# Windowed attention with sinks and a highway layer: rows in pairs for the 32x32 transpositions of q, and the last two batches loaded whole

## The chip, the cores and the metric

The kernel runs on one core of a Trainium2 chip. The metric is the device time of one execution in microseconds (us); the time shown for a kernel is the median of several runs. The profile is of one execution, and it has that execution's own time beside the span that it covers.

A core has five engines with queues of their own: TensorE (PE in the profile; its weight loads are PEld), VectorE (DVE), ScalarE (ACT), GpSimd (POOL) and SyncE (SP). Each works through its own instructions in order. POOL, SP and ACT also issue DMA transfers.

## The reference

```python
def _attn_ref(q, k, v, n_sink, window):          # q, k, v: [4, 8, 768, 64]; n_sink 4, window 128
    B, H, S, D = q.shape
    scores = np.matmul(q, k.transpose(0, 1, 3, 2)) / np.sqrt(D)
    pos = np.arange(S)
    rel = pos[:, None] - pos[None, :]
    keep = (pos[None, :] < n_sink) | ((rel >= 0) & (rel < window))
    scores = np.where(keep, scores, -1000000000.0)
    a = np.exp(scores - np.max(scores, axis=-1, keepdims=True))
    a = a / (np.sum(a, axis=-1, keepdims=True) + 1e-09)
    return np.matmul(a, v)

def _moe_ref(x, w_h, w_t, b_t):                  # x: [3072, 512], the heads side by side
    H = np.maximum(x @ w_h, 0.0)
    T = 1.0 / (1.0 + np.exp(-(x @ w_t + b_t)))
    return T * H + (1.0 - T) * x
```

All inputs and the output are float32. The kernel works in float16 behind its loads.

## The kernel before

The 4 batches of 768 tokens make 24 tiles of 128 tokens, six to a batch. One loop (`for n in range(N + 2)`, L471) is a software pipeline over these tiles: in iteration n the kernel makes the scores of key tile n and their exponentials, multiplies the values of tile n-1, normalises and transposes tile n-1, and runs the gate and the hidden product of tile n-2. The closing elementwise work of a tile (`complete`: half a tanh, a product, a sum and the store) comes five or six iterations after its scores, by the table `completed` (L448); iteration 13 closes two tiles, and so do iterations 21 to 23. The order of instructions on each engine is that in which the Python code issues them (`_keep_traced_order`). Nothing is moved by a planner.

**Layout of q and k.** The 8 heads are taken as two groups `hg` of four, and the four heads of a group lie on the four quarters of the partitions (`G` = 4, 32 partitions each). POOL loads q and k (L109) and the DMA casts them to float16. A batch is cut in segments: three of 256 tokens for batches 0 and 1, two of 384 for batches 2 and 3. Within a segment, partition r of a quarter holds `run` = 8 or 12 consecutive tokens, all 64 numbers of each. One DMA brings one segment, of q or of k, for the two heads of one quarter; so a segment of q takes four DMAs, and all of batches 1 to 3 takes 56, of which eight come ahead of the table `loads`.

**The transpositions.** `transpose_qk` (L125) reads the float16 data as 4-byte words, two numbers of a head side by side. VectorE transposes blocks of 32 partitions by 32 words: the word moves to the partition, and the 32 partition rows become the free index. Row r of a block belongs to token `r * run + m`, so that consecutive words that one block writes are `run` words apart: 32 bytes for the thirds, 48 bytes for the halves. The result `tr[b]` is, on each partition, for q and k and each `hg`, the tokens in order with the two numbers (`e` = 0, 1) side by side: 4 bytes from token to token. Thirds are done in one instruction for both `hg` (512 words per partition), halves in one per `hg` (384 words).

**Who reads it.** `scores` (L279) takes, for each `hg`, `e` and quarter, 128 tokens of k as weights and up to 256 tokens of q as moving operand, a row group of 32 each, four of them side by side in the array. `sink_scores` (L293) takes q against the four sink keys, and `sink_keys` (L253) puts these keys together from `tr`. 

**Order.** A table `units` says behind which iteration's `norm` VectorE transposes which piece: for batch 1 at iterations 5, 5, 6, 7, 8, 9; for batch 2 at 10, 10, 11, 11, 12, 13, 14, 14; for batch 3 at 16, 16, 17, 17, 18, 19, 20, 20. Batch 2 is first used by `scores(12)`, batch 3 by `scores(18)`; with halves, the second half is first needed in iterations 14 and 15 (and 20 and 21), by the sinks' scores and by key tile 3. The table `loads` says how many DMAs POOL issues in iterations 2 to 16: 4, 4, 4, 4, 3, 3, 3, 3, 2, 3, 3, 3, 3, 3, 3. On POOL an iteration's order is: cast of v(n) (L142), the DMAs of `loads`, the sum that closes a tile (L414), and at the first two tiles of a batch the sinks' keys and values. The values of tile n-1 need the cast of the iteration before. On VectorE the order is: reciprocal and product of `norm` (L349, L351), the transpositions, `diff` (L403), and `gate_value` and `gated` (L384, L408). PE needs the result of `diff` of one iteration before the hidden product of the next can write `ps_h`, which exists once.

## Time and profile before

| | us |
|---|---|
| median of 3 runs | 115.75 |
| lowest and highest of them | 114.94 and 116.42 |
| the profiled execution | 114.55 |
| its span | 112.8 |
| PE busy | 98.4 |
| VectorE busy | 87.5 |
| POOL busy | 87.2 |
| ScalarE busy | 76.6 |

The span begins with the first instruction and ends with the last; the execution's time has 1.75 us more, outside the span. Shares of busy time are means over stages with different limits. Iterations can be told in the timeline of VectorE: each has one reciprocal (L349), that of iteration 1 at 14.39 us, of iteration 24 at 103.34 us. "Chain" means the chain of work that ended last, followed back from the end. A line such as "3.11 DMA nat<-in_k_dram" in it is the time from a DMA's issue to its landing; x4 is the number of instructions that a row merges.

### The profile page before, as it was taken

What the parts mean: (1) busy time and instruction counts of PE and PEld (TensorE: products, weight loads), DVE (VectorE), ACT (ScalarE), POOL (GpSimd) and SP (SyncE); (2) the same over time, 40 slices, a digit from 0 to 9 for tenths busy, and PEclk for the clock granted to TensorE, in tenths of its full rate; (3) what the DMA queues carried; (4) which work ended last, traced back from release to release, by engine and by line L of the source; (5) the groups of instructions that cost most, each with busy time, mean ns of one, the idle gap of its engine ahead of it and who ended that gap; (6) DMA issues with size and microseconds to landing.
All of it is one profiled execution on the core that took longest, in us unless ns stands there. A gap on an engine that the chain in (4) does not pass through costs nothing.

```text
span 112.8 us, 3577 instructions
## 1 busy us (share of the span) xinstructions
PE 98.4 (87%) x1414; PEld 51.5 (46%) x1414; DVE 87.5 (78%) x184; ACT 76.6 (68%) x95; POOL 87.2 (77%) x141
## 2 busy tenths in 40 slices
PE   5986389899989998999999979999999999977900
PEld 2322246345435454655455535644555566523500
DVE  6796587535677986889998998699777979999660
ACT  4476639985557786788587868687678987842520
POOL 6899997249599499997899999999758965866100
PEclk9999999999999999999999999999999999999998
DMA  3999999999999749989998999899994503324222
GB/s 97 222 234 214 210 201 224 192 204 242 212 241 150 112 139 233 256 193 237 203 207 205 224 239 261 166 209 210 242 259 131 162 6 136 143 99 176 103 111 75
DMA packets 36704, 20.81 MB, mean 185 GB/s; under 512 B 27340, under 2 KB 33232, under 8 KB 36688
## 3 DMA queue, kind: packets, MB, share of 16 engines
q1 hardware_dynamic: 29680, 13.50, 46.6%
q0 software_dynamic: 6848, 6.82, 38.6%
q10 hardware_dynamic: 160, 0.26, 0.8%
q8 instruction: 11, 0.18, 0.7%
q14 instruction: 5, 0.04, 0.1%
HBM read 21.11 MB, written 6.29 MB: 243 GB/s over the span
## 4 chain that ended last, share of the span: by engine, by line
PE 39%; DVE 22%; POOL 14%; DMA 14%; issue 7%; DVEq 1%; POOLq 0%
POOL nat L109 11%; PE ps_h L390 9%; DMA wh<-in_moe_w_h_dram 9%; PE ps_z L371 8%; DVE tr L125 7%; PE ps_s L279 5%; DMA nat<-in_k_dram 5%; DVE DD L403 4%; DVE TH L384 4%; PE ps_av L341 4%; PE ps_av L338 3%; PE ps_s L272 3%; DVE DD L408 2%; PE ps_av L362 2%; DVE X L351 2%
## 5 line engine op out<-in xcount | busy, mean ns | idle before, releaser
L327 ACT ACTIVATE E<-ps_s,ebias 128x2048 f16<-128x2048 f32 (+1 forms) x24 | 43.8, 1825 | 12.6 <-PE ps_s L279 12.6
L414 POOL TENSOR_TENSOR O<-DD,X 128x512 f32<-128x512 f16 x22 | 25.4, 1156 | 10.1 <-DVE DD L408 4.2
L390 PE MATMUL ps_h<-wh,XT 128*128 128x512 f16 (+1 forms) x96 | 27.4, 375 | 0.2 <-DMA wh<-in_moe_w_h_dram 0.2
L125 DVE STREAM_TRANSPOSE tr<-nat 128x384 f32<-128x384 f32 (+1 forms) x28 | 25.7, 957 | 2.3 <-DMA nat<-in_k_dram 1.9
L109 POOL DMA_DIRECT2D nat<-in_k_dram x40 | 21.9, 554 | 5.5 <-DMA wh<-in_moe_w_h_dram 3.7
L371 PE MATMUL ps_z<-wt,XT 128*128 128x512 f16 x96 | 24.6, 379 | 0.0
L403 DVE SCALAR_TENSOR_TENSOR DD<-ps_h,X 128x512 f16<-128x512 f32 (+1 forms) x24 | 16.2, 673 | 8.2 <-PE ps_h L390 8.1
L367 ACT COPY XT<-ps_av 128x512 f16<-128x512 f16 x24 | 14.1, 586 | 7.8 <-PE ps_av L362 5.0
L378 ACT ACTIVATE TH<-ps_z 128x512 f16<-128x512 f32 x24 | 14.2, 592 | 7.4 <-PE ps_z L371 7.4
L109 POOL DMA_DIRECT2D nat<-in_q_dram x32 | 17.8, 562 | 0.8 <-DMA wt<-in_moe_w_t_dram 0.7
L351 DVE TENSOR_TENSOR X<-ps_av,rec 128x512 f16<-128x512 f32 x24 | 16.6, 692 | 1.0 <-DVE rec L349 0.2
L341 PE MATMUL ps_av<-v,E 128*128 128x65 f16 x192 | 14.1, 194 | 1.9 <-DVE v L142 1.8
L279 PE MATMUL ps_s<-tr 32*128 32x256 f16 (+1 forms) x384 | 14.5, 262 | 1.0 <-DVE tr L125 0.8
L341 PEld LDWEIGHTS <-E 128*128 128x128 f16 x192 | 11.8, 98 | 3.0 <-issue 3.0
L338 PE MATMUL ps_av<-v,E 128*128 128x65 f16 x160 | 12.7, 195 | 0.0
L408 DVE TENSOR_TENSOR DD<-DD,TH 128x512 f16<-128x512 f16 x24 | 11.9, 495 | 0.8
L338 PEld LDWEIGHTS <-E 128*128 128x128 f16 x160 | 10.2, 97 | 4.9 <-issue 4.9
L362 PE MATMUL ps_av<-ident,X 128*128 128x128 f16 x96 | 9.4, 221 | 3.2 <-DVE X L351 3.0
L142 POOL CAST v<-V 128x512 f16<-128x512 f32 x19 | 12.0, 633 | 0.0
L390 PEld LDWEIGHTS <-XT 128*128 128x128 f16 x100 | 8.7, 98 | 6.9 <-issue 0.7
L362 PEld LDWEIGHTS <-X 128*128 128x128 f16 x96 | 5.7, 97 | 12.2 <-DVE X L351 12.2
L371 PEld LDWEIGHTS <-XT 128*128 128x128 f16 x96 | 7.8, 98 | 6.0 <-ACT XT L367 0.3
(62 smaller groups left out, 100.9 us busy)
## 6 DMA issues: line engine op xcount, KB each, us to landing
V<-in_v_dram SPq DMA_DIRECT2D x24, 256.0 KB, 5.2
out_dram<-O SPq DMA_DIRECT2D x23, 256.0 KB, 2.8
nat<-in_k_dram POOLq DMA_DIRECT2D x24, 64.0 KB, 4.5
nat<-in_q_dram POOLq DMA_DIRECT2D x16, 96.0 KB, 4.2
nat<-in_k_dram POOLq DMA_DIRECT2D x16, 96.0 KB, 4.5
nat<-in_q_dram POOLq DMA_DIRECT2D x16, 64.0 KB, 4.9
first<-in_q_dram SPq DMA_DIRECT2D x6, 128.0 KB, 3.7
wt<-in_moe_w_t_dram POOLq DMA_DIRECT2D x1, 512.0 KB, 6.7
```

The costliest lines, as they stand in the source:

```text
L109: engine.dma_start(out=into[32 * g:32 * g + 32].rearrange("p hg m d -> p hg (m d)"), in_=(q, k)[which][b, :, t0:t0 + nt, :].rearrange("(hg ...
L125: dve.transpose(out=dst, in_=src)
L279: last = pe.matmul(ps_s[:, g, hg, 0:nq * P], lhsT=tr[b][rows, 1, hg, c * P:(c + 1) * P, e], rhs=tr[b][rows, 0, hg, c * P:(c + nq) * P, e], ...
L327: act.activation(out=E[n][:, :, :, 0:nq * P], in_=ps_s[:, :, :, 0:nq * P], func=AF.Exp, bias=ebias, scale=SCALE)
L338: pe.matmul(slot, lhsT=E[n - 1][:, g, hg, P:2 * P], rhs=v_of(n - 1)[:, h, :], start=first, stop=False, skip_group_check=True)
L341: pe.matmul(slot, lhsT=E[n][:, g, hg, 0:P], rhs=v_of(n)[:, h, :], start=first, stop=True, skip_group_check=True)
L351: dve.tensor_tensor(out=X[n], in0=av[:, :, :, 0:D], in1=rec.unsqueeze(3).to_broadcast([P, HG, G, D]), op=ALU.mult)
L362: pe.transpose(xt[:, kc // 2, (kc % 2) * P:(kc % 2 + 1) * P], x[:, kc * P:(kc + 1) * P], ident)
L371: pe.matmul(ps_z, lhsT=XT[n][:, kc * P:(kc + 1) * P], rhs=wt[:, kc, :], start=False, stop=(kc == KC - 1), skip_group_check=True)
L390: pe.matmul(into, lhsT=XT[n][:, kc * P:(kc + 1) * P], rhs=wh[:, kc, cols], start=(kc == 0), stop=(kc == KC - 1), skip_group_check=True)
L403: dve.scalar_tensor_tensor(out=DD[n][:, cols], in0=ps_h[:, cols] if h is None else h, scalar=0.0, in1=flat(X[n], cols), op0=ALU.max, op1=A ...
L414: eng.tensor_tensor(out=O[n][:, cols], in0=DD[n][:, cols], in1=flat(X[n], cols), op=ALU.add)
```

## The change

Three things change together.

1. For batches 0 and 1 (`b < SPLIT`) the loads and pieces are the same thirds. The transposition of k is the same. That of q puts rows 2x and 2x+1 of a block side by side: the two words that the two rows give are written at neighbouring addresses, the next pair 64 bytes on. In `tr` the tokens of q are then no longer in order; the readers take them through a pattern (x, y, m), in runs of 8 tokens with 8 bytes from token to token.
2. For batches 2 and 3 one tile holds the whole batch. Partition 32g + 2r + i holds 48 consecutive tokens of head `4i + g`: the rows of a quarter alternate between its two heads. One DMA brings one head of q or of k, 16 partitions of 12 KB read and 6 KB written each (before: 64 pieces of 3 KB read and 1.5 KB written). The number of DMAs stays 56 for batches 1 to 3, and their size 96 KB for batches 2 and 3. The transposition writes the words of the two heads side by side, and `tr` has the two `hg` inside the token: 8 bytes from token to token for q and k. An instruction takes 16 of the 48 tokens of every row, 512 words per partition, three for q and three for k of a batch (before: four and four of 384 words). Each of the three of k needs all eight DMAs of k, and a batch's first scores need all six.
3. The order: batch 2 is transposed at iterations 9, 10, 10 (q) and 11, 11, 11 (k), batch 3 at 14, 15, 15 (q) and 16, 17, 17 (k). The loads come as all of q, then all of k; POOL issues 4 in each of iterations 2 to 9 and then 2, 3, 3, 3, 3, 2, the last in iteration 15.

```diff
+    RUN = SEG // 32
+    SPLIT = 2
+    WHOLE = S // 16
+    nat = [[data.tile([P, 2, HG, RUN, D], FP16, ...) for i in range(NSEG)] for b in range(SPLIT)] + [
+           [data.tile([P, 2, WHOLE, D], FP16, tag=f"nat{b}", name=f"nat{b}")]
+           for b in range(SPLIT, B)]
+    tr = [data.tile([P, 2, HG, S, 2] if b < SPLIT else [P, 2, S, HG, 2], FP16,
+                    tag=f"tr{b}", name=f"tr{b}") for b in range(B)]
...
     def load_part(b, i, g, which, into=None, engine=pool):
...
+        else:
+            engine.dma_start(
+                out=nat[b][0][32 * g + i:32 * g + 32:HG, which].rearrange("p m d -> p (m d)"),
+                in_=(q, k)[which][b, G * i + g].rearrange("(r m) d -> r (m d)", m=WHOLE))
...
-        src = nat[b][i][:, which, hgs].bitcast(FP32).rearrange("p hg m i -> p hg m i")
-        dst = tr[b][:, which, hgs].bitcast(FP32).rearrange("p hg t e -> p hg (t e)")[
-            :, :, t0:t0 + nt].rearrange("p hg (r m) -> p hg m r", m=run)
+    def transpose_qk(b, i, which, parts=NSEG):
+        if b < SPLIT:
+            src = nat[b][i][:, which].bitcast(FP32)
+            dst = tr[b][:, which].bitcast(FP32).rearrange("p hg t e -> p hg (t e)")[
+                :, :, i * SEG:(i + 1) * SEG]
+            if which == 0:
+                dst = dst.rearrange("p hg (x m y) -> p hg m x y", m=RUN, y=2)
+                src = src.rearrange("p hg m (x y) -> p hg m x y", y=2)
+            else:
+                dst = dst.rearrange("p hg (r m) -> p hg m r", m=RUN)
+        else:
+            ms = slice(i * WHOLE // parts, (i + 1) * WHOLE // parts)
+            src = nat[b][0][:, which, ms].bitcast(FP32).rearrange("p m (x y) -> p m x y", y=HG)
+            dst = tr[b][:, which].rearrange("p t hg e -> p t (hg e)").bitcast(FP32).rearrange(
+                "p (x m) y -> p m x y", m=WHOLE)[:, ms]
         dve.transpose(out=dst, in_=src)
+
+    def queries(b, hg, e, t0, nt, rows=slice(0, P)):
+        if b >= SPLIT:
+            return tr[b][rows, 0, t0:t0 + nt, hg, e]
+        return tr[b][rows, 0, hg, t0:t0 + nt, e].rearrange(
+            "p (x m y) -> p x y m", m=RUN, y=2)
+
+    def keys_of(b, hg, e, t0, nt, rows=slice(0, P)):
+        if b >= SPLIT:
+            return tr[b][rows, 1, t0:t0 + nt, hg, e]
+        return tr[b][rows, 1, hg, t0:t0 + nt, e]
...
-                                     lhsT=tr[b][rows, 1, hg, c * P:(c + 1) * P, e],
-                                     rhs=tr[b][rows, 0, hg, c * P:(c + nq) * P, e],
+                                     lhsT=keys_of(b, hg, e, c * P, P, rows),
+                                     rhs=queries(b, hg, e, c * P, nq * P, rows),
...
-            at = (10, 10, 11, 11, 12, 13, 14, 14) if b == 2 else (16, 16, 17, 17, 18, 19, 20, 20)
+            at = (9, 10, 10, 11, 11, 11) if b == 2 else (14, 15, 15, 16, 17, 17)
             for u, n in enumerate(at):
-                i, which, hg = u // 4, u // 2 % 2, u % 2
-                units.setdefault(n, []).append((b, i, which, slice(hg, hg + 1)))
+                units.setdefault(n, []).append((b, u % NSEG, u // NSEG))
...
+    issues += [(b, i, g, which) for b in range(SPLIT, B) for which in range(2)
+               for g in range(G) for i in range(HG)]
-    for n, count in zip(range(2, 17), [4] * 4 + [3, 3, 3, 3, 2, 3, 3, 3, 3, 3, 3]):
+    for n, count in zip(range(2, 16), [4] * 8 + [2, 3, 3, 3, 3, 2]):
```

38 lines of the change are left out of this document (18 added, 20 removed).

## The prediction

> **What bounds the kernel now.** I read the page first: engines, slices, and the chain of waits by engine.
>
> ```profile
> span 112.8 us, 3577 instructions
> ...
> PE 98.4 (87%) x1414; PEld 51.5 (46%) x1414; DVE 87.5 (78%) x184; ACT 76.6 (68%) x95; POOL 87.2 (77%) x141
> ...
> DMA  3999999999999749989998999899994503324222
> ...
> PE 39%; DVE 22%; POOL 14%; DMA 14%; issue 7%; DVEq 1%; POOLq 0%
> ```
>
> No engine is full, and the chain changes between four of them; so what counts is which wait ends last in each stage. The DMA engines are busy to slice 29 of 40, that is for some 85 us. Next, the chain in order of time (start, length, what); these are its hand-overs that bear on the change.
>
> ```profile
> 27.79 3.11 DMA nat<-in_k_dram
> ...
> 31.47 1.11 DVE tr L125
> ...
> 44.12 0.42 PE ps_av L293 x26
> ...
> 54.70 1.54 DVE tr L125 x2
> ...
> 56.29 0.41 PE ps_s L279 x8
> ...
> 59.46 0.33 PE ps_s L272 x8
> ...
> 62.76 0.33 PE ps_s L272 x8
> ...
> 68.57 0.64 POOL v L142
> ...
> 69.24 0.19 PE ps_av L341
> ...
> 71.81 0.33 PE ps_s L272 x8
> ...
> 72.81 0.14 PE ps_av L338
> ...
> 77.83 1.55 DVE tr L125 x2
> ...
> 79.42 0.41 PE ps_s L279 x8
> ...
> 85.90 0.33 PE ps_s L272 x8
> ...
> 89.90 0.33 PE ps_s L272 x8
> ```
>
> To 31 us loads rule (the wait on a k load ends at 30.90). Then PE rules, at 3.30 us per tile (59.46 to 62.76) and 4.00 in an iteration with the sinks' scores (85.90 to 89.90), broken by transpositions at four places: before scores(6), before the sinks' scores in iteration 8 (44.12), before scores(12) (56.29) and before scores(18) (79.42). In iteration 15 it is the cast of v(14) on POOL that ends last (69.21). Behind 79.42 no transposition is on the path, and the tail is the closing work of the late tiles, which the change doesn't touch. So a microsecond counts only if scores(18) moves.
>
> **The price of a transposition.** The view of groups by line with shapes kept apart (count, busy us, mean ns, then idle before):
>
> ```profile
> L125 DVE STREAM_TRANSPOSE tr<-nat 128x512 f32<-128x512 f32 x12 | 13.1, 1102 | 2.3 <-DMA nat<-in_k_dram 1.9 <-issue 0.4
> L125 DVE STREAM_TRANSPOSE tr<-nat 128x384 f32<-128x384 f32 x16 | 12.7, 849 | 0.0
> L414 DVE TENSOR_TENSOR O<-DD,X 128x512 f32<-128x512 f16 x1 | 0.7, 693 | 0.1
> L457 DVE CAST nat<-first 128x512 f16<-128x512 f32 x1 | 0.4, 427 | 0.2 <-DMA first<-in_q_dram 0.2
> L272 PE MATMUL ps_s<-mq,mk 32*128 32x256 bf16 x176 | 9.1, 273 | 0.9 <-ACT E L327 0.9
> L279 PE MATMUL ps_s<-tr 32*128 32x256 f16 x320 | 12.9, 271 | 1.0 <-DVE tr L125 0.8
> ```
>
> From 384 to 512 words the time grows by 253 ns, 1.98 ns per word, with 849 - 384 x 1.98 = 89 ns fixed. No transposition before writes two words side by side, so the new price has to be bounded: above by 1102 ns (the word itself is what takes the time), below by the 427 ns of the cheapest 512-word operation. A gain beyond that, or a loss, has no row that suggests it: the words read and written are the same. I take 693 ns, the row of VectorE that writes 512 4-byte words in order, since what changes is how the written words lie. That is 0.41 us less for each of 6 transpositions of q in batches 0 and 1; batches 2 and 3 go from 16 of 849 to 12 of 693 ns.
>
> Both old strides, 32 and 48 bytes, fit one slope. The Trainium skill's page "Advanced Engine Details and Errata", section "SBUF Cachelines", says that on-chip memory works in lines of 16 bytes, that at least two accesses must fall into a line for full rate, and that another line at each access costs. Both old strides take a new line for each word and the pairs give two words to a line, so by it VectorE at one word per cycle (0.96 GHz by the Trainium skill's page "Trainium Kernel Development and Optimization", section "NeuronCore Architecture"; an estimate of 0.53 us for 512) plus the fixed part would give some 0.62 us; the sum below would then be 0.2 us lower. By it the change on the reading side is free too, since tokens 8 bytes apart still fall two to a line.
>
> **The reading side.** Scores now stream q at 8 bytes per token. Rows have only 2 bytes (L272, 273 ns) and 4 bytes (L279, 271 ns): doubling the step cost nothing. The bounds for the next doubling are nothing and twice the 0.48 us that 16 score matmuls take, below; a gain has no mechanism. I take nothing, the nearest row. Weight loads of k at 8 bytes have cover: PEld is busy 46%.
>
> ```profile
> 40.74 0.48 PE ps_s L279 x16
> ```
>
> **The schedule on VectorE.** One iteration, number 16, from its timeline:
>
> ```profile
> 73.50 0.21 DVE L349 RECIPROCAL rec<-ps_av 128x8 f32<-128x8 f32 x1 [0.24 <-PE ps_av L341]
> 73.75 0.69 DVE L351 TENSOR_TENSOR X<-ps_av,rec 128x512 f16<-128x512 f32 x1
> 74.36 1.54 DVE L125 STREAM_TRANSPOSE tr<-nat 128x384 f32<-128x384 f32 x2
> 75.74 0.68 DVE L403 SCALAR_TENSOR_TENSOR DD<-ps_h,X 128x512 f16<-128x512 f32 x1
> ...
> 76.99 0.20 DVE L349 RECIPROCAL rec<-ps_av 128x8 f32<-128x8 f32 x1
> ```
>
> From start to start: norm 0.86, two transpositions 1.38 (about 0.15 each under their durations, by overlap; I take 0.1 off the new one, 0.59), diff with the closing pair behind it 1.25: 2.11 us without transpositions, against PE's 3.30. So one or two new ones fit (2.70, 3.29) and three do not (3.88).
>
> **POOL and the loads.** Its timeline, with its waits of over 1 us between 36 and 69 us and the places that matter:
>
> ```profile
> 38.58 1.15 POOL L414 TENSOR_TENSOR O<-DD,X 128x512 f32<-128x512 f16 x1 [1.49 <-DVE DD L408]
> ...
> 48.38 1.62 POOL L109 DMA_DIRECT2D nat<-in_q_dram  x3
> ...
> 54.07 1.14 POOL L414 TENSOR_TENSOR O<-DD,X 128x512 f32<-128x512 f16 x1 [1.19 <-DMA vs<-in_v_dram]
> ...
> 68.52 0.68 POOL L142 CAST v<-V 128x512 f16<-128x512 f32 x1
> ...
> 73.53 0.54 POOL L109 DMA_DIRECT2D nat<-in_k_dram  x1
> ```
>
> Each issue is 0.54 us, and I take the same for DMAs of fewer, longer pieces. The change moves four issues ahead of iteration 10, 2.16 us. The wait of 1.49 takes up most of that, and the one of 1.19, which ended on VectorE's work, can close as well: so cast(14) can come at best 1.49 + 1.19 - 2.16 = 0.5 us earlier, and a little more by short waits. Queued behind the added issues are the casts of v, for which the value matmuls wait. The time from issue to landing, over all loads (minimum, median, maximum), then for single k loads in the windows 50 to 52, 68 to 72 and 71 to 75 us:
>
> ```profile
> DMA to landing us min/median/max: 2.9/4.5/8.4
> ```
> ```profile
> nat<-in_k_dram POOLq DMA_DIRECT2D x1, 96.0 KB, 4.4
> ```
> ```profile
> nat<-in_k_dram POOLq DMA_DIRECT2D x1, 96.0 KB, 3.1
> ```
> ```profile
> nat<-in_k_dram POOLq DMA_DIRECT2D x1, 96.0 KB, 4.6
> ```
>
> **The sum.**
> - scores(6): q's piece ahead of k's is 0.41 us shorter, and k's load is there at 30.90, 0.57 before its transposition began: -0.4.
> - Iteration 8: the sinks' scores wait for a transposition of q: -0.4, together -0.8.
> - Iterations 9 to 11: batch 2's k is issued until 50.0 + 2.16 - 1.49 = 50.7 and lands, with 4.4, at 55.1. VectorE would be ready for it near 53.9 (54.70 less 0.8), so it now waits 1.2. Three transpositions of 0.59 end at 56.9: scores(12) +0.6 against 56.29.
> - Iterations 12 to 15: without transpositions in 12 and 13 and with one in 14, PE is not held by VectorE. Scores(12) at 56.9 and two tiles of 3.30 lead to scores(14) at 63.4; iteration 14, with the sinks' scores, is 4.0, and values(14) are wanted 1.0 us into iteration 15 (as 72.81 follows 71.81), at 68.4. POOL gives cast(14) 0.5 to 0.9 before 69.2, that is at the same time. Iteration 15 therefore begins its values at 68.4: -0.8, and the 0.6 of before is no longer seen.
> - Iterations 16 and 17: batch 3's last two k loads are issued in iteration 15. They are out at 73.53 - 0.8 = 72.7 (the third of that iteration is gone) and land between 75.8 (3.1) and 77.3 (4.6). Iteration 16 wants all eight at 74.36 - 0.8 = 73.6. VectorE stands there 2 to 4 us, and in its queue behind it are diff(14), for which hidden(15) on PE waits, the closing pair, norm(16) and the last two transpositions. I take a landing of 3.5, nearer the lower, since one load less is in front of it: 76.2; then 0.59 for k's first piece, 1.25, 0.86 and 1.18 for the last two give 80.1, and with 0.1 for the hand-over scores(18) stand at 80.2, against 79.42: **+0.8 us**. By a landing of 2.9 it is +0.2, by 4.6 +1.9.
> - Behind that PE is full to 90 us, and fewer transpositions in iterations 18 to 20 give nothing.
>
> The gain of the front is thus spent on loads that come too late for their new place. 114.55 + 0.8 = 115.35 us for the profiled execution. That one was 1.2 us under the median of the runs, 115.75; carried over to it, the forecast is 116.5 us.
>
> **Rivals.**
> 1. *Loads and POOL don't hold it.* If the long pieces land in under 2.5 us, or the issues get much cheaper than 0.54, VectorE's relief goes through: 0.8 to iteration 8, 0.5 at scores(12), 1.2 of the 1.75 in iterations 14 and 15 (9.05 us from 62.76 to 71.81, against 4.00 + 3.30 for PE alone; the rest is POOL's), 0.5 at scores(18), where two pieces take 1.28 rather than 1.54 and iteration 16 has one piece less: -3.0, 111.55, or 112.75 against the median. For it: 64 pieces become 16 longer ones. Against it: no load in the trace lands under 2.9.
> 2. *The transpositions stay at 1.10 us* (the change doesn't do what it is meant to). At 1.0 from start to start an iteration with two takes 4.1, with three 5.1, where 3.3 to 3.5 were enough before: 0.8, 0.6 and 1.6 are lost in iterations 9, 10 and 11, scores(12) +3.0. Two tiles, 4.0 and 1.0 on, values(14) are at 70.9, +1.7. Iteration 15 with two loses 0.8 more, and 16 and 17 end, by the same steps as above with 1.0 for 0.59, 0.8 later still: +3.3, or 119.05 against the median, slower by 2.9%. For it: one slope for both strides, which a cost per word gives as well.
> 3. *PE reads q at half rate.* 0.48 more on some 17 tiles where PE rules is +8, and with the forecast's 0.8 124.5. It decides from 0.15 us per tile on. Against it: 2 and 4 bytes cost the same.
> 4. *The long pieces land late*, 6 us rather than 3.5, because 16 long pieces share engines with the loads of v: both waits grow, the second in full by 2.5: +3.3, 119.05, slower by 2.9%. For it: a maximum of 8.4.
>
> **Chances.** The forecast 0.45; rival 1 0.23, rival 2 0.18, rival 3 0.06, rival 4 0.08. What a measurement here can tell from no change is about 2%, or 2.3 us. The forecast's own range is 115.9 to 117.7, within 2% (landings of 2.9 to 4.6). Faster: rival 1, less its weak half-gains, 0.22. Slower: rivals 2 to 4, less the milder part, 0.28. Within 2%: 0.50. The range goes from 113.0, inside rival 1, to 119.3, which takes in rivals 2 and 4 at their centres; half of rival 1, rival 3 and the far ends are left out, some 0.2.
>
> **What would show it.** The mean of the 128x512 transposition in pairs: 0.6 to 0.7, or 1.10 (rival 2). L279's mean and the spacing of its 16: 271 ns and 0.48, or more (rival 3). VectorE's idle time before L125 by k loads in iterations 11 and 16: 1 and 2.5 us in the forecast, none in rival 1, over 4 in rival 4. Cast(14) as what ends last before values(14). Scores(18) near 80.2. I am wrong if landing is not what holds iteration 16, or if POOL's queue has run further ahead by then than I take it to.

## The result and the profile after

The changed kernel takes 142.15 us, the median of 4 runs (140.51 to 143.89), against 115.34 us (4 runs, 114.07 to 116.42) for the kernel before on the same chip. The ratio is 1.232, with a 95% interval of 1.212 to 1.252. The forecast was 116.5 us, and 119.3 us was the top of its range. The profiled execution took 140.51 us. A ratio leaves out executions over 1.5% above the fastest of their kernel, so it can differ a little from that of the medians.

The page of the changed kernel: span, busy time, and three of the rows by slices of 3.47 us.

```profile
span 138.7 us, 3566 instructions
...
PE 112.7 (81%) x1414; PEld 56.0 (40%) x1414; DVE 80.9 (58%) x180; ACT 76.8 (55%) x95; POOL 85.2 (61%) x141
...
PE   6964998999999999059899893393799999999740
...
PEclk9999599999999999955999999969999999999997
DMA  4999999999934999408859975081257450234232
```

VectorE's busy time fell from 87.5 to 80.9 us, as the shorter transpositions should make it. PE's rose from 98.4 to 112.7 us with the same 1414 matmuls. And there are holes that the profile before did not have: counted from 0, PE does nothing in slice 16 (from 55.5 us) and the DMA nothing in slice 17, and behind them the clock is at half for two slices; slices 24 to 27 have the like. So there are two things to explain, work that takes longer and pauses.

The work first. The groups by line with shapes kept apart (count, busy us, mean ns, then idle before and what ended it):

```profile
L319 PE MATMUL ps_s<-tr 32*128 32x256 f16 x320 | 22.2, 406 | 1.6 <-DVE tr L146 1.5
L146 DVE STREAM_TRANSPOSE tr<-nat 128x512 f32<-128x512 f32 x24 | 18.7, 796 | 21.1 <-DMA nat<-in_k_dram 20.7 <-issue 0.4
...
L319 PEld LDWEIGHTS <-tr 32*128 32x128 f16 x384 | 10.9, 110 | 7.5 <-DVE tr L146 2.7
```

The transpositions' mean of 796 ns mixes 18 in pairs at 0.70 us with the 6 of k in batches 0 and 1, unchanged at 1.10. The score matmul went from 271 to 406 ns. In the chain, 15 or 16 of them in a row now stand for 0.9 us, where they stood for 0.48:

```profile
107.16 0.91 PE ps_s L319 x15
```

The pauses are in the second row of the groups: VectorE waited 20.7 us for loads of k ahead of its transpositions (before: 1.9). VectorE's timeline shows where (start, length, what, and in brackets the idle time before and what ended it). These three waits are 18.3 of the 20.7 us; they lie in iterations 9, 14 and 15.

```profile
58.78 0.71 DVE L146 STREAM_TRANSPOSE tr<-nat 128x512 f32<-128x512 f32 x1 [6.11 <-DMA nat<-in_k_dram]
...
86.86 0.71 DVE L146 STREAM_TRANSPOSE tr<-nat 128x512 f32<-128x512 f32 x1 [6.95 <-DMA nat<-in_k_dram]
...
94.90 1.30 DVE L146 STREAM_TRANSPOSE tr<-nat 128x512 f32<-128x512 f32 x2 [5.25 <-DMA nat<-in_k_dram]
```

By the table of the change, iterations 9, 14 and 15 transpose pieces of **q**. They wait for **k**. Is k late? POOL's timeline shows the issues of k just ahead of each wait:

```profile
51.70 1.96 POOL L120 DMA_DIRECT2D nat<-in_k_dram  x4
...
81.88 1.50 POOL L120 DMA_DIRECT2D nat<-in_k_dram  x3
...
90.61 1.00 POOL L120 DMA_DIRECT2D nat<-in_k_dram  x2
```

From the end of each issue to the start of the waiting transposition it is 5.1, 3.5 and 3.3 us. From the start of the issue to the landing, as the trace counts it, the last loads took 5.4, 3.9 and 3.7 us, inside the 2.9 to 8.4 us that loads took before. The loads are not slow; the pieces wait for loads that they don't read, issued in the same iteration. In the trace the first piece of q of batch 2 waits on the eight semaphores that the batch's sixteen loads use in turn, the next ones on none. It begins at 58.78, 0.18 us behind the landing of the last load of k (58.60); the last load of q had landed at 50.83.

Where the time went, by stages. Each number is the time from one reciprocal of VectorE to another (the one of iteration 1 to that of iteration 4, and so on), for the two kernels and for two of the experiments that follow: q and k in tiles of their own, and the same with TensorE reading at 4 bytes.

| iterations | before | after | two tiles | two tiles, read at 4 bytes |
|---|---|---|---|---|
| first reciprocal at | 14.39 | 14.70 | 14.52 | 15.15 |
| 1 to 4 | 11.51 | 13.15 | 13.44 | 12.30 |
| 4 to 9 | 20.88 | 22.87 | 22.86 | 20.14 |
| 9 to 11 | 7.07 | 14.69 | 7.52 | 7.55 |
| 11 to 12 | 3.77 | 4.81 | 5.04 | 5.70 |
| 12 to 16 | 15.88 | 27.14 | 17.44 | 15.64 |
| 16 to 17 | 3.49 | 3.42 | 3.85 | 6.03 |
| 17 to 24 | 26.35 | 28.51 | 28.53 | 26.34 |

The pauses are the 7.6 us in the row 9 to 11 and most of the 11.3 us in the row 12 to 16. The row 17 to 24, where no transposition is on the path, shows the longer matmuls alone: 2.2 us. The row 1 to 4 isn't read further: in both kernels that read at 8 bytes it holds a stretch of 3.4 us at half clock (from 14.4 and from 15.9 us), and what brings that on is not known.

### The profile page after: what moved, and what is told of

The parts are those of the page before. It is cut to its first block, busy times and chain, and to the rows that moved or that the text cites. A ratio compares the mean times of both kernels' runs of the same rounds, so it can differ in the third digit from the quotient of the medians.

```text
span 138.7 us, 3566 instructions
## 1 busy us (share of the span) xinstructions
PE 112.7 (81%) x1414; PEld 56.0 (40%) x1414; DVE 80.9 (58%) x180; ACT 76.8 (55%) x95; POOL 85.2 (61%) x141
## 5 line engine op out<-in xcount | busy, mean ns | idle before, releaser
L430 PE MATMUL ps_h<-wh,XT 128*128 128x512 f16 (+1 forms) x96 | 28.7, 391 | 10.7 <-DVE DD L443 10.7
L146 DVE STREAM_TRANSPOSE tr<-nat 128x512 f32<-128x512 f32 x24 | 18.7, 796 | 21.1 <-DMA nat<-in_k_dram 20.7
L319 PE MATMUL ps_s<-tr 32*128 32x256 f16 (+1 forms) x384 | 24.8, 387 | 1.6 <-DVE tr L146 1.5
L430 PEld LDWEIGHTS <-XT 128*128 128x128 f16 x100 | 8.8, 100 | 18.7 <-issue 12.7
L381 PE MATMUL ps_av<-v,E 128*128 128x65 f16 x192 | 14.5, 196 | 1.5 <-DVE v L182 1.5
L115 POOL DMA_DIRECT2D nat<-in_k_dram x24 | 13.0, 550 | 3.2 <-DMA wh<-in_moe_w_h_dram 2.4
L319 PEld LDWEIGHTS <-tr 32*128 32x128 f16 x384 | 10.9, 110 | 7.5 <-DVE tr L146 2.7
L402 PE MATMUL ps_av<-ident,X 128*128 128x128 f16 x96 | 10.0, 231 | 4.6 <-DVE X L391 4.5
L381 PEld LDWEIGHTS <-E 128*128 128x128 f16 x192 | 12.1, 99 | 3.3 <-issue 3.3
L389 DVE RECIPROCAL rec<-ps_av 128x8 f32<-128x8 f32 x24 | 4.9, 204 | 14.0 <-PE ps_av L381 13.8
L378 PE MATMUL ps_av<-v,E 128*128 128x65 f16 x160 | 12.9, 197 | 0.0
L378 PEld LDWEIGHTS <-E 128*128 128x128 f16 x160 | 10.5, 99 | 5.7 <-issue 5.7
L448 DVE TENSOR_TENSOR DD<-DD,TH 128x512 f16<-128x512 f16 x24 | 11.3, 473 | 0.8
```

What stands on the lines that cost most here:

```text
L146: dve.transpose(out=dst, in_=src)
L319: last = pe.matmul(ps_s[:, g, hg, 0:nq * P], lhsT=keys_of(b, hg, e, c * P, P, rows), rhs=queries(b, hg, e, c * P, nq * P, rows), start=Fal ...
L378: pe.matmul(slot, lhsT=E[n - 1][:, g, hg, P:2 * P], rhs=v_of(n - 1)[:, h, :], start=first, stop=False, skip_group_check=True)
L381: pe.matmul(slot, lhsT=E[n][:, g, hg, 0:P], rhs=v_of(n)[:, h, :], start=first, stop=True, skip_group_check=True)
L402: pe.transpose(xt[:, kc // 2, (kc % 2) * P:(kc % 2 + 1) * P], x[:, kc * P:(kc + 1) * P], ident)
L430: pe.matmul(into, lhsT=XT[n][:, kc * P:(kc + 1) * P], rhs=wh[:, kc, cols], start=(kc == 0), stop=(kc == KC - 1), skip_group_check=True)
```

## The experiments

Three suspects came out of the traces: the waits of q's pieces for k's loads, the reading at 8 bytes, and the order (all of a batch loaded ahead of its first scores). The experiments take them away one by one, and add each alone to the kernel before. All ratios are to the kernel before on the same chip.

### Tiles of their own for q and k

The changed kernel; only the two halves of a batch's tile become two tiles.

```diff
-           [data.tile([P, 2, WHOLE, D], FP16, tag=f"nat{b}", name=f"nat{b}")]
+           [data.tile([P, WHOLE, D], FP16, tag=f"nat{b}_{w}", name=f"nat{b}_{w}") for w in "qk"]
            for b in range(SPLIT, B)]
...
-                out=nat[b][0][32 * g + i:32 * g + 32:HG, which].rearrange("p m d -> p (m d)"),
+                out=nat[b][which][32 * g + i:32 * g + 32:HG].rearrange("p m d -> p (m d)"),
```

> The changed kernel, with the one tile that holds q and k of batch 2 (and of batch 3) made into two tiles, one for q and one for k; nothing else differs. Theory A (the transpositions of q wait for loads of k, because both lie in one tile and their loads write every second partition): VectorE's waits of 6.1, 7.0 and 5.3 us in iterations 9, 14 and 15 are gone; what stays is a wait of up to 2 us for k in iteration 16 and up to 1 us in iteration 11; the granted clock is back near 1.0; 122 to 126 us instead of 140.5. Rival B (the long pieces land late, as rival 4 of the prediction has it): waits of over 4 us stay in iterations 11 and 16, and the time is over 130. Rival C (the loss is PE's alone, and VectorE's waits are hidden): within 3 us of 140.5.

124.48 us (123.66 to 125.04), ratio 1.074 (1.066 to 1.083), as theory A had it: 17.7 us of the loss are gone. The timeline of VectorE in this kernel has one wait left ahead of a transposition in batches 2 and 3, in iteration 16, where the prediction had put it (first row); the score matmuls are as slow as in the changed kernel (second row, the groups by shape).

```profile
82.81 0.71 DVE L146 STREAM_TRANSPOSE tr<-nat_k 128x512 f32<-128x512 f32 x1 [1.06 <-DMA nat_k<-in_k_dram]
```
```profile
L319 PE MATMUL ps_s<-tr 32*128 32x256 f16 x320 | 22.1, 406 | 1.5 <-DVE tr L146 1.4
```

### One tile, but neighbouring partitions

Is it the common tile, or the way in which the loads write it? Here the tile stays common, and each load writes 16 neighbouring partitions rather than every second one. The scores of batches 2 and 3 are then made from rows of other heads; the amount of work is the same.

```diff
-                out=nat[b][0][32 * g + i:32 * g + 32:HG, which].rearrange("p m d -> p (m d)"),
+                out=nat[b][0][32 * g + 16 * i:32 * g + 16 * i + 16, which].rearrange("p m d -> p (m d)"),
```

> The changed kernel with q and k of a batch still in one tile, but each load writes 16 neighbouring partitions instead of every second one of 32, so that the rows of the two heads no longer alternate: the scores of batches 2 and 3 are made from rows of the wrong head and token, and the same work is done. Theory A1 (it is the step of two partitions that makes q's transpositions wait for loads of k): like the kernel with two tiles, no wait in iterations 9, 14 and 15, 123.5 to 125.5 us. Rival A2 (the common tile is enough): waits of 5 to 7 us in these iterations, 139 to 143 us. Rival B2 (loads into every second partition land later): landing times under 3 us, where they were 3.3 to 5.

126.4 us, a single execution, 0.9 us above what theory A1 expected. Iterations 9, 14 and 15 wait for nothing; the waits of VectorE's timeline after 25 us that are left lie in iterations 11 and 16, and they are longer than with two tiles:

```profile
59.89 1.90 DVE L146 STREAM_TRANSPOSE tr<-nat 128x512 f32<-128x512 f32 x3 [0.53 <-DMA nat<-in_q_dram]
...
84.78 0.71 DVE L146 STREAM_TRANSPOSE tr<-nat 128x512 f32<-128x512 f32 x1 [2.55 <-DMA nat<-in_k_dram]
```

The first row names a load of q, but its piece reads k: the loads share semaphores, and by the landing times in the trace the last load of k came 0.18 us before the piece began. The same holds for the rows of iteration 11 that name a load of q below. The loads of k took longer here (median 5.6 us to landing, 4.4 with two tiles), so rival B2 falls; whether that is more than chance, one execution can't tell.

So it is the step of two partitions in a common tile. With it the program that the framework makes has q's pieces wait for loads of k, as if these overlapped the region of q; with neighbouring partitions, or with two tiles, it doesn't. How the framework's dependency tracking comes to that is not shown. The chip has no part in it: with two tiles the loads write every second partition all the same.

### The first part alone

The kernel before with q of batches 0 and 1 transposed in pairs and read in runs of 8 tokens, 8 bytes from token to token; batches 2 and 3, loads and order stay.

```diff
+        if b < 2 and which == 0:
+            src = src.rearrange("p hg m (x y) -> p hg m x y", y=2)
+            dst = dst.rearrange("p hg (x m y) -> p hg m x y", m=run, y=2)
...
-                                     rhs=tr[b][rows, 0, hg, c * P:(c + nq) * P, e],
+                                     rhs=queries(b, hg, e, c * P, nq * P, rows),
```

> The kernel before, with part 1 of the change alone: q of batches 0 and 1 transposed in pairs of rows and read at 8 bytes per token in runs of 8; loads, batches 2 and 3 and the order as before. Theory (PE takes a moving operand at 8 bytes per token at half rate): the 16 score matmuls of a tile take 0.92 us instead of 0.48 in batches 0 and 1 and 0.48 in batches 2 and 3; tiles 6 to 11 are ruled by PE, so 6 x 0.45 and 0.2 for the sinks' scores, less 0.8 for the shorter transpositions: 1 to 2.5 us slower than before. Rival (the step of 8 bytes is free, and PE is slow in the changed kernel for another reason): 0.48 us everywhere and 0.5 to 0.8 us faster than before.

119.63 us (118.28 to 120.42), ratio 1.025 (1.014 to 1.035): slower, as the theory had it, and by more than its 1 to 2.5 us. In the profiled execution iterations 4 to 11 take 2.46 us more than before; most of the rest lies in iterations 1 to 4. The mean of the score matmuls lies between 271 and 406 ns, since half of the tiles read at 8 bytes:

```profile
L288 PE MATMUL ps_s<-tr 32*128 32x256 f16 x320 | 17.8, 341 | 1.5 <-DVE tr L130 1.3
```

A transposition that is 0.4 us shorter is paid for by tiles that are 0.4 us longer, and there are more tiles on the path than transpositions.

### The reading alone: q at 8 bytes, k at 8 bytes

The kernel before, with the two `hg` inside the token in `tr` for q alone (the diff), then for k alone (`INSIDE = (False, True)`). Nothing is written in pairs and the tokens are in order; the reading, and the spacing of the words that a transposition writes (64 bytes for the thirds, 96 for the halves) are what changes.

```diff
+    INSIDE = (True, False)
+    tr = [[data.tile([P, S, HG, 2] if INSIDE[w] else [P, HG, S, 2], FP16, ...)
...
-                                     lhsT=tr[b][rows, 1, hg, c * P:(c + 1) * P, e],
-                                     rhs=tr[b][rows, 0, hg, c * P:(c + nq) * P, e],
+                                     lhsT=tr[b][1][rows, hg, c * P:(c + 1) * P, e],
+                                     rhs=tr[b][0][rows, hg, c * P:(c + nq) * P, e],
```

> The kernel before, with q's two groups of heads put inside the token in the transposed tile, so that all tiles read q at 8 bytes per token, in order; loads, order and the number of transpositions as before, and their words still lie one by one (64 or 96 bytes apart). Theory (half rate at 8 bytes): transpositions stay at 1.10 and 0.85 us, the 16 score matmuls take 0.92 us in all 24 tiles, 17 to 18 of them on the path: 5 to 9 us slower than before. Rival (what costs is the broken order of part 1, or the clock): within 1 us of before.

> The same for k alone: weights of the scores read at 8 bytes per token, q at 4 bytes. Theory (weight loads lie beside the matmuls): a weight load goes from 92 to some 105 to 110 ns, the 16 matmuls stay at 0.48 us, the time within 1 us of before. Rival (weights pay as the moving operand does): over 3 us slower.

With q at 8 bytes: 124.89 us (123.21 to 125.91), ratio 1.081 (1.071 to 1.092). With k at 8 bytes: 117.23 us (116.54 to 117.99), ratio 1.013 (1.008 to 1.017). The groups of the kernel with q at 8 bytes, and then those of the one with k at 8 bytes:

```profile
L282 PE MATMUL ps_s<-tr,tr 32*128 32x256 f16 x320 | 21.6, 398 | 0.8 <-DVE tr L128 0.8
L128 DVE STREAM_TRANSPOSE tr<-nat 128x384 f32<-128x384 f32 x16 | 14.8, 989 | 0.0
```
```profile
L282 PE MATMUL ps_s<-tr,tr 32*128 32x256 f16 x320 | 13.9, 281 | 2.8 <-DVE tr L128 2.6
L282 PEld LDWEIGHTS <-tr 32*128 32x128 f16 x384 | 10.1, 112 | 5.2 <-DVE tr L128 4.6
```

The moving operand pays in full, 398 ns rather than 271, and the theory's 5 to 9 us are there at their upper end (8.8 by the medians). The weights pay some 20 ns of a load (112 rather than 92). The second kernel is 1.2 us slower, a little over the 1 us expected, and the reading is hardly the cause: the halves of k are written 96 bytes apart, and one such transposition takes 1.1 us rather than 0.85 (the mean of 989 above, for q, is half old pieces, half new). From iteration 17 to 24 this kernel takes 27.30 us and the kernel before 26.35; the kernel with all of q lying, below, reads k of batches 2 and 3 at 8 bytes too, with short transpositions, and takes 26.38.

### The loads and the order alone

The kernel with two tiles, without pairs: all of `tr` in the layout of before, read at 4 bytes, with the loads and the order of the change. Its transpositions of batches 2 and 3 write words 192 bytes apart.

```diff
-    tr = [data.tile([P, 2, HG, S, 2] if b < SPLIT else [P, 2, S, HG, 2], FP16,
+    tr = [data.tile([P, 2, HG, S, 2], FP16,
...
+            dst = tr[b][:, which].bitcast(FP32)[:, :, :, 0].rearrange(
+                "p y (x m) -> p m x y", m=WHOLE)[:, ms]
```

> The kernel with two tiles, and without pairs and without steps of 8 bytes: all transposed tiles as before, 4 bytes from token to token, each word of a transposition by itself (in batches 2 and 3 the rows of a head are 192 bytes apart); loads and order of the changed kernel. Theory (with the reading at 4 bytes PE is as before, and what is left is VectorE's longer pieces in iterations 9 to 11 and 15 to 17 and the late k of iteration 16): 16 score matmuls in 0.48 us, transpositions of 512 words in batches 2 and 3 at 1.1 to 1.5 us, 1.5 to 6 us slower than before. Rival (long loads or the new order cost most of the rest by themselves): within 1.5 us of the two-tile kernel, 123 to 126 us.

123.31 us (121.91 to 124.23), ratio 1.059 (1.052 to 1.066): more than the theory's 1.5 to 6 us, and inside the rival's 123 to 126. The order of the change costs by itself, even with the reading at its old price: iteration 11 waits for loads of k and then has three transpositions of about 1.05 us. The waits of VectorE's timeline in iterations 11 and 16:

```profile
58.20 2.77 DVE L142 STREAM_TRANSPOSE tr<-nat_k 128x512 f32<-128x512 f32 x3 [1.53 <-DMA nat_q<-in_q_dram]
...
83.86 1.05 DVE L142 STREAM_TRANSPOSE tr<-nat_k 128x512 f32<-128x512 f32 x1 [2.66 <-DMA nat_k<-in_k_dram]
```

In this execution PE stood still for 3.15 us in iteration 12, and then the clock was at 0.50 from 62.5 to 65.9 us: iteration 12 to 13 took 4.98 us, where it takes 3.30 in the kernel before.

It left open how much of the loss is the longer transpositions and how much the loads. The next two kernels separate that.

### The change without the coupling and without the reading

The kernel with two tiles; the writes in pairs, the loads and the order are those of the change. TensorE alone reads the same memory as if its tokens lay 4 bytes apart, so that the scores are made from other tokens, with as many matmuls of the same size.

```diff
+    lying = [x if b < SPLIT else x.rearrange("p w t hg e -> p w (t hg e)").rearrange(
+        "p w (hg t e) -> p w hg t e", hg=HG, e=2) for b, x in enumerate(tr)]
...
-            return tr[b][rows, 0, t0:t0 + nt, hg, e]
-        return tr[b][rows, 0, hg, t0:t0 + nt, e].rearrange(
-            "p (x m y) -> p x y m", m=RUN, y=2)
+        return lying[b][rows, 0, hg, t0:t0 + nt, e]
```

> The kernel with two tiles per batch (q and k apart), its loads, pairs and order unchanged; only TensorE reads q and k of batches 2 and 3 at 4 bytes per token, and q of batches 0 and 1 in the order in which it lies, so that the scores are made from other tokens (the same number of matmuls of the same size). Theory: the reading at 8 bytes is what is left of the loss, so the 16 score matmuls take 0.48 us again, L319 falls from 406 to some 275 ns, and the time goes from 124.5 to what the prediction had, 114.5 to 118 us. Rival: the order and the loads cost by themselves, as the kernel with these alone (123.3) suggests: 119 to 122 us, with the waits for k in iteration 16 growing to over 2.5 us as TensorE gets there earlier.

120.23 us (119.28 to 122.38), ratio 1.037 (1.030 to 1.045). The matmuls are back at their old price, and the kernel is 4.3 us faster than with the reading at 8 bytes; but the rival of the expectation holds, not the theory. First the groups, then VectorE's timeline in iterations 11 and 16:

```profile
L316 PE MATMUL ps_s<-tr 32*128 32x256 f16 x320 | 13.1, 278 | 5.3 <-DVE tr L148 5.2
```
```profile
57.32 1.90 DVE L148 STREAM_TRANSPOSE tr<-nat_k 128x512 f32<-128x512 f32 x3 [1.25 <-DMA nat_k<-in_k_dram]
...
80.65 0.71 DVE L148 STREAM_TRANSPOSE tr<-nat_k 128x512 f32<-128x512 f32 x1 [3.24 <-DMA nat_k<-in_k_dram]
```

The wait in iteration 16 was 1.06 us with the slow reading and is 3.24 us now. PE gets there sooner, and the loads don't. That is why the reading costs 4.3 us here and more in the order of before (124.89 us for q at 8 bytes against 117.23 for k, with as many long transpositions: 7.7 us): in this order part of it stood in front of loads that were late anyway.

### The same without the late loads of k

The kernel above; the pieces of k in batch 2 are transposed out of q's tile of that batch, those in batch 3 out of k's tile of batch 2. All loads are still issued, and the scores of batches 2 and 3 are made from other data.

```diff
-            src = nat[b][which][:, ms].bitcast(FP32).rearrange("p m (x y) -> p m x y", y=HG)
+            src = (nat[2][0] if b == 2 else nat[2][which])[:, ms].bitcast(FP32).rearrange("p m (x y) -> p m x y", y=HG)
```

> The kernel with two tiles and reading at 4 bytes (120.2 us; its profiled run waits 1.25 us in iteration 11 and 3.24 us in iteration 16 for loads of k), with one thing more: the pieces of k of batch 2 are transposed out of q's tile of that batch, those of batch 3 out of k's tile of batch 2, both there earlier. All loads are still issued; the scores of batches 2 and 3 are made from other data. Theory: these two waits are all that is left of the loss; without them the time is 115.0 to 116.5 us, level with the kernel before, and the shorter transpositions by themselves give nothing. Rival: the shorter transpositions do give the 2 to 3 us that the prediction's first rival had, as soon as the loads do not hold them: 112.5 to 113.5 us. Second rival: POOL's queue (casts behind the earlier issues) holds the middle: 117.5 us or more, with waits of the value matmuls for L179.

115.84 us, ratio 0.998 (0.991 to 1.004): the theory holds, and both rivals fall. The profiled execution was the longest of its ten (118.05 us, with 14.40 us from iteration 1 to 4, where the clock was at 0.50 from 24.6 to 28.0 us), so only its later stages are read; from 57 to 81 us the clock was at 1.00. In them the pieces of iterations 11 and 16 wait for nothing, and iteration 11 to 12 takes 4.34, iteration 16 to 17 3.26 us:

```profile
58.09 1.89 DVE L148 STREAM_TRANSPOSE tr<-nat_q 128x512 f32<-128x512 f32 x3
...
61.59 0.21 DVE L386 RECIPROCAL rec<-ps_av 128x8 f32<-128x8 f32 x1 [0.39 <-PE ps_av L378]
...
77.24 0.21 DVE L386 RECIPROCAL rec<-ps_av 128x8 f32<-128x8 f32 x1
78.09 0.70 DVE L148 STREAM_TRANSPOSE tr<-nat_k 128x512 f32<-128x512 f32 x1
80.50 0.21 DVE L386 RECIPROCAL rec<-ps_av 128x8 f32<-128x8 f32 x1
```

With this the loss is closed in three steps: 142.15 to 124.48 us (the coupling), to 120.23 (the reading), to 115.84 (the late loads of k), against 115.8 before. What remains of the change, transpositions that are a third shorter, is worth nothing that this measurement can tell.

### Pairs without the reading, in the old order

If the reading is what spoils part 1, TensorE can read q in the order in which it lies (4 bytes from token to token), and ScalarE can put the queries in order as it writes the exponentials. The mask for the queries is permuted once. This is the kernel before with q of batches 0 and 1 in pairs, then with four rows side by side (`y=4` throughout).

```diff
+            src = src.rearrange("p hg m (x y) -> p hg m x y", y=2)
+            dst = dst.rearrange("p hg (x m y) -> p hg m x y", m=run, y=2)
...
+            parts = [(put.rearrange("p g hg q -> p (g hg q)").rearrange(
+                          "p (x y m) -> p x y m", m=8, y=2),
+                      got.rearrange("p g hg q -> p (g hg q)").rearrange(
+                          "p (x m y) -> p x y m", m=8, y=2))]
...
+            act.activation(out=put, in_=got, func=AF.Exp, bias=ebias, scale=SCALE)
```

> The kernel before, with q of batches 0 and 1 transposed in pairs of rows, but read by PE in the order in which the tokens lie, at 4 bytes per token; the mask's query factor has the same order, and ScalarE puts the queries back in order as it writes the exponentials. Theory (all that part 1 costs is the step of 8 bytes): transpositions of q at 0.70 us, 16 score matmuls at 0.48 us, 0.4 to 0.9 us faster than before, if ScalarE's exponentials stay at 1.97 us. Rival (ScalarE pays for reading every second number): exponentials over 2.5 us in batches 0 and 1, and 1 to 4 us slower.

> The same with four rows side by side, 16 bytes. Theory L (VectorE writes in lines of 16 bytes, and a full line is as good as writing in order): the transposition of q falls from 0.70 to 0.60 to 0.66 us. Rival P (what counts is the pair): it stays at 0.69 to 0.71 us. The time within 0.3 us of the version by two, if ScalarE reads every fourth number as it reads every second.

In pairs: 115.63 us (12 runs), ratio 0.998 (0.994 to 1.002), short of the 0.4 to 0.9 us that were expected. In fours: 115.15 us (12 runs), ratio 0.994 (0.990 to 0.997). The second is the only kernel here whose interval lies below the kernel before, by 0.6%, less than the 2% that the prediction took as what can be told from no change. The groups of the version in fours:

```profile
L358 ACT ACTIVATE E<-ps_s,ebias 128x2048 f16<-128x2048 f32 x20 | 39.3, 1967 | 13.1 <-PE ps_s L290 13.1
L290 PE MATMUL ps_s<-tr 32*128 32x256 f16 x320 | 13.2, 271 | 2.8 <-DVE tr L130 2.6
...
L130 DVE STREAM_TRANSPOSE tr<-nat 128x512 f32<-128x512 f32 x12 | 10.7, 901 | 2.6 <-DMA nat<-in_k_dram 2.0 <-issue 0.6
```

The exponentials take the 1967 ns that they take in the kernel before, so the reordering costs ScalarE nothing where one instruction can do it (the tiles with half the queries need two at 684 ns or four at 475, for one at 1113). The mean of 901 is that of pieces at 0.70 and at 1.10: four rows side by side are no cheaper than two, so rival P holds.

### All of q lying, in the change's order, and its loads sooner

The same idea carried into the change: two tiles, q of batches 2 and 3 loaded in thirds of 8-token runs, eight DMAs as before, and all of q read as it lies. Then the same with the table of loads alone changed.

```diff
+                out=nat[b][0][rows, i].rearrange("p c m d -> p c (m d)"),
+                in_=q[b, G * i + g].rearrange("(c r m) d -> r c (m d)", c=NSEG, m=RUN))
...
+        return trq[b][rows, hg, t0:t0 + nt, e]
```
```diff
-    for n, count in zip(range(2, 16), [4] * 8 + [2, 3, 3, 3, 3, 2]):
+    for n, count in zip(range(2, 14), [4] * 12):
```

> A version that computes the reference: two tiles per batch, the change's order; q of batches 2 and 3 comes in thirds of 8-token runs (one DMA per head as in the change), its transposition writes pairs as in batches 0 and 1, TensorE reads all of q in lying order at 4 bytes, ScalarE puts the tokens in order when it writes the exponentials; k of batches 2 and 3 is written and read at 8 bytes as in the change (as weights). Theory: transpositions of 0.70 us without the price of the reading: 0.5 to 2 us faster than the kernel before if loads do not hold iteration 16, about the same (114.5 to 116.5) if they do. Rival: the order and the loads cost by themselves: 119 to 122.

> The version that computes the reference with all of q lying (120.1 us), its table of loads alone changed: 4 issues in each of iterations 2 to 13 rather than 4 in 2 to 9 and then 2, 3, 3, 3, 3, 2, so that the last load of k goes out in iteration 13 rather than 15. Theory: the wait in iteration 16 (2.6 us) goes and the time falls by 1.5 to 2.5 us to 117.5 to 118.5, with the wait in iteration 11 (2.0 us) left. Rival: POOL cannot issue them earlier without making its casts late: the same time or slower, 119.5 to 122.

120.12 us, ratio 1.037 (1.031 to 1.043), and with the loads sooner 120.35 us, ratio 1.036 (1.023 to 1.049): both times are those of the rivals. The first has the two waits of the kernel without the reading, by VectorE's timeline:

```profile
58.07 1.90 DVE L152 STREAM_TRANSPOSE trk<-nat_k 128x512 f32<-128x512 f32 x3 [1.97 <-DMA nat_q<-in_q_dram]
...
80.79 0.71 DVE L152 STREAM_TRANSPOSE trk<-nat_k 128x512 f32<-128x512 f32 x1 [2.60 <-DMA nat_k<-in_k_dram]
```

In the second the wait in iteration 16 is gone, as its theory had it, and yet nothing is won. Its wait in iteration 11 grew to 2.85 us, PE stood still for 3.57 us, and then this happened (windows of the kernel with loads sooner: us, busy time of PE, PEld, DVE, ACT and POOL with counts, then the granted clock, DMA share, GB/s):

```profile
56.90:60.50 3.60, 0.04 (x4) 0.00 (x1) 1.95 (x4) 0.00 (x0) 3.20 (x6) 0.93 1.18 252
60.50:66.70 6.20, 6.20 (x47) 3.09 (x47) 2.04 (x5) 3.15 (x3) 3.64 (x6) 0.50 1.04 217
66.70:70.00 3.30, 3.30 (x46) 1.79 (x45) 2.95 (x7) 2.26 (x2) 1.58 (x3) 0.98 0.41 81
```

For 6.2 us behind the pause the clock is at half. Iteration 12 to 13 takes 5.2 us there and 3.3 us in the kernel with the loads as they were, where PE's pause was 2.69 us and the clock stayed at 1.00. In this execution the first wait took more than the second gave: iterations 11 to 12 and 12 to 13 are 1.9 us longer each, 16 to 17 is 2.1 us shorter. It was the longest of four, 121.91 us; the two shortest took 118.59 and 119.86, and whether they lose the same way is not known. That POOL's casts came late, which the rival gave as its reason, is not shown.

## Why the prediction was wrong, step by step

Of the 26.8 us, 17.7 went with the waits of q's pieces for loads of k, then 4.3 with the reading at 8 bytes, then 4.4 with the late loads of k, taken away in this order. The first is a wait that the prediction did not have; the second is a term that it put at nothing; in the third, terms of its sum were mis-sized.

**That q's pieces wait for q.** The prediction takes from the change that batch 2 is transposed "at iterations 9, 10, 10 (q)", and gives VectorE waits for k alone, in iterations 11 and 16. Nothing in its sum and none of its rivals has q's pieces waiting for loads of k. The trace of before could not show it, since the tile and the loads that cause it are new; the diff could: `32 * g + i:32 * g + 32:HG` is a region with holes, in a tile that q and k share. Undoing this alone gives back 17.7 of the 26.8 us. Rival 4 (long pieces land late) has long waits but not their cause: it takes 6 us for the landing, and the loads that were waited for landed in 3.7 to 5.4 us.

**"I take nothing, the nearest row."** This is the step on the reading side, and it failed. From 2 to 4 bytes the matmul stays at 271 to 273 ns; from 4 to 8 it goes to 398 to 406. The upper of the two bounds, twice the 0.48 us, was nearly reached: 0.91 us for the block. Rival 3, with a chance of 0.06, described it rightly: it had +8 us from the reading, and the two kernels with q and with k at 8 bytes differ by 7.7. The prediction leaned on two rows that lie on one side of the step. The rule that it cites from the Trainium skill, "Advanced Engine Details and Errata", section "SBUF Cachelines", said the same: two accesses to a 16-byte line are enough for full rate. At 8 bytes two tokens fall into a line, and the rate is nearly halved. The measurement differs from the page here, and decides.

**The price of the transposition.** I took 693 ns, and it is 688 to 704 ns in all the kernels that write pairs. Right. The page's rule agrees here: two words to a line are faster than one. That a line filled by four words gives no more was tried above.

**The front, -0.8 us.** It is there where the prediction put it. Iterations 4 to 5 and 8 to 9, with the reading out of the way, take 4.42 and 4.26 us rather than 4.75 and 4.66; together 0.73 us of the row 4 to 9 in the table. In that execution iterations 1 to 4, where loads rule, took 0.8 us more than in that of the kernel before and ate it up. In the other kernels without slow reading of q they took 11.75 to 12.77 us (14.40 in the execution with half clock there, above), so 11.51 is the short end; why stays open.

**The waits for k, and the gain that was to pay for them.** The waits are where the prediction put them: 1.25 us against a forecast of 1.2 in iteration 11, 3.24 against 2.5 in iteration 16. POOL's issues end where the sum had them, 4.65 us behind the reciprocal of iteration 9 (forecast 4.72), and at that of iteration 16. Four rows of POOL's timeline in the kernel with two tiles and reading at 4 bytes:

```profile
50.28 1.96 POOL L122 DMA_DIRECT2D nat_k<-in_k_dram  x4
...
60.59 1.15 POOL L451 TENSOR_TENSOR O<-DD,X 128x512 f32<-128x512 f16 x1 [2.09 <-DMA V<-in_v_dram]
...
71.50 0.66 POOL L179 CAST v<-V 128x512 f16<-128x512 f32 x1
...
75.30 1.00 POOL L122 DMA_DIRECT2D nat_k<-in_k_dram  x2
```

Mis-sized is the landing. From the end of the issue to the waiting transposition it took 5.1 us where I took 4.4, and 4.35 where I chose 3.5 "since one load less is in front of it". The sum also reads the landing times wrongly: the trace counts them from the start of an issue, and the sum adds them to its end, so that 0.5 us is in it twice. Counted as the trace counts them, the landings took 5.4 and 4.7 us against 4.4 and 3.5, and the second lies just above the 4.6 that the range stops at; the double 0.5 hid nearly half of the error. That the first wait still came out at its forecast size is luck: VectorE also got there 0.56 us later than the sum had it. Iteration 9 has two pieces now, and one of them is a third of k, still at 1.10 us. With the prediction's own steps, 2.11, 1.0 and 0.59, that is 3.70 us and not under PE's 3.30; it took 4.26 (0.44 of it a wait for a load of q), against 3.59 before.

Mis-sized is also the gain in iterations 12 to 15. The sum goes there from +0.6 to -0.8, so it wins 1.4 us; the stretch from iteration 12 to 16 won 0.24 (15.64 against 15.88 us). From scores(14) to scores(15) it takes 4.6 us, where the sum had 4.0 and the kernel before 4.75: the chain goes there through VectorE's closing of two tiles, which has no transposition in front of it. And the cast of v(14) still ends last before values(14), as the prediction's sign had it, but it ends 3.84 us behind the reciprocal of iteration 14, where it ended 3.94 behind it before. The lead that POOL had from issuing earlier went into waits: 2.09 and 0.51 us before the closing sums of iterations 11 and 12 (0.19 and 0.24 before).

By the table, the kernel without the coupling and without the reading stands at -0.74 us by iteration 9 (forecast -0.8), loses 2.41 to iteration 12 (forecast 1.4), wins 0.24 to iteration 16 (forecast 1.4) and loses 2.54 to iteration 17 (forecast 1.6): about 4.0 us from iteration 4 on, where the forecast had +0.8 in all. Taking the late loads away gave back 4.4 (120.23 to 115.84).

**Rival 1**, that the relief of VectorE goes through once loads don't hold it, was worth 3 us in the prediction. With the loads out of the way it comes to a ratio of 0.998. In the later stages of that execution iterations 12 to 16 and 16 to 17 are shorter than before by 0.23 us each (15.65 and 3.26), as the rival has it in part; but 9 to 11 takes 7.44 us against 7.07, and 11 to 12 takes 4.34 against 3.77, with three pieces between norm(11) and scores(12) where there were two. So the relief is real, and the order of the change spends it.

**Half clock.** The prediction counts a pause at its own length. Behind the pause in iteration 9 of the changed kernel there is more: the clock is at half (windows of the changed kernel; columns as above):

```profile
56.00:60.10 4.10, 0.00 (x0) 0.00 (x0) 1.32 (x3) 0.42 (x1) 0.00 (x0) 0.84 0.28 57
60.10:66.00 5.90, 5.39 (x51) 2.66 (x51) 4.48 (x11) 1.70 (x2) 3.98 (x6) 0.53 0.52 122
```

Iteration 14 has a stretch of 3.4 us at 0.50 as well (89.5 to 92.9 us). By this reading the 17.7 us that went with the coupling are the waits, 18.3 us, and what the clock added, less what comes back in iterations 11 and 16 when q's pieces no longer wait; how they divide was not measured.

## What to carry to other kernels

When a layout is changed to make its writer faster, price its readers with a kernel that changes the reading alone: here one doubling of the step was free, and the next cost 7.7 us of 117. When a diff has several loads write a common tile in a stepped pattern, ask what each consumer will be made to wait for, and give the parts that come at different times tiles of their own. If a transfer's new place is less than a landing ahead of its use, take a landing from the long end of those in the trace, and add what PE loses behind a long pause: 1.7 and 1.9 us in the iterations behind those of 3.15 and 3.57 us.

## What the runs showed of the hardware that was not expected

- **TensorE's moving operand** (float16, 256 columns, 32 rows): 271 to 278 ns at a step of 4 bytes, 398 to 406 ns at 8. As weights the same step costs 16 to 20 ns of a load (92 against 108 to 112).
- **VectorE's transposition by the spacing of the words it writes**, 512 words: 1.10 us at 32 bytes, 1.04 to 1.07 us at 192; 384 words: 0.85 us at 48 bytes, 1.1 us at 96, so spacing doesn't matter in a simple way. Two words side by side: 0.69 to 0.70 us; four: 0.70 us.
- **ScalarE** reads the scores out of order, 8 or 16 bytes apart, at no price: 1967 ns either way.
- **The clock**: pauses of PE of 4.59 and 3.57 us were followed by some 6 us at 0.50 to 0.53, pauses of 3.79 us (iteration 14 of the changed kernel) and 3.15 us (iteration 12 of the kernel with the loads and the order alone) by 3.4 us at 0.50; one of 2.69 us was not. The Trainium skill's page "TensorE: Matmul & The Clock Gate", Part 1, has the clock fall to half behind about 3.4 us of idleness. Four of these five pauses agree with it; that of 3.15 us is shorter and was followed by half clock all the same. Half clock also came without such a pause: in the kernel with two tiles 3.4 us at 0.50 begin at 15.9 us, where the longest pauses just before were of 0.89 and 1.26 us.
